# A gated linear recurrence and a low-rank mixer: the first batch's outputs from the diagonal squares, its block totals in place, a bitwise sign, and another order

## The chip, the cores and the metric

The kernel runs on one core of one Trainium2 chip. The metric is device time in microseconds, the median of a few executions; less is better. Engines are named as the profile names them: PE (matmul), PEld (its weight loads), DVE (vector), ACT (scalar), POOL (GpSimd), SP (the queue that issues most DMAs).

## The reference

Two blocks follow each other, all in f32. The first is a complex gated recurrence for 4 batches, 8 heads, 768 steps and 48 channels:

```python
scale = np.minimum(mag, 0.999) / (mag + 1e-06)      # mag = |a_re + i a_im|
a_re_n, a_im_n = (a_re * scale, a_im * scale)
for t in range(S):
    new_re = ar * S_re - ai * S_im                  # ar, ai: a_re_n, a_im_n at t, per channel
    new_im = ar * S_im + ai * S_re
    S_re, S_im = (new_re + outer(k_t, v_t), new_im)
    y[t] = q_t @ S_re
```

Its outputs, heads side by side, are `x` of shape (4, 768, 384) for the second:

```python
h = x.T @ U @ V                                     # per batch, along the sequence; rank 32
u = x + h.T
out = u + np.maximum(u @ w_ch1, 0.0) @ w_ch2        # 384 -> 1536 -> 384
```

## The kernel before

The sequence is cut into chunks of 128 steps, 6 for each batch, 24 in all. Chunks go in groups of two (12 groups); group 0 is worked one chunk at a time. Chunks 0 to 5 are the first batch, groups 0 to 2. From group 3 on (`SPLIT`) sums over time are made from an f32 that is split in two f32r parts.

For each group, `gates` computes the log magnitude (`GL`) and the angle of `a` with ACT's tables and DVE. Part of that is a sign of `a_re` in the tile `n`: for group 0 by DVE as +-0.5, for the others by ACT's Sign. `turns_of` multiplies `n` by arctan minus pi/4 and then scales the product to turns and adds 0.25 (DVE for group 0, ACT for the others). PE sums over time with the triangle `prefix` (`ph`). `within` makes the decay weights inside a chunk (`es`, `ef`). `totals` makes sums of logs over blocks, 32 for each channel (`tot`), which ACT turns into factors. For two heads at once these land in `E`, two heads one under the other, and four DMAs a group place them in `T`, whose rows are the channels once for the cosine half and once for the sine half (rows 0 to 47 and 64 to 111).

For each chunk, `prep` weighs q and k, multiplies them by cosine and sine (`QKC`), transposes them on PE (`tr`), and ACT copies them to `QK`. `chain` computes the chunk's causal weights. `inner` products of q and k in diagonal squares of 32 steps are selected by masks into `DG` (128 x 8 heads x 32). Four DMAs place the squares of `DG` in `AT`, which holds squares of 64. The part of such a square under its diagonal (`corners`) is copied there by ACT, four copies of 32 rows. `dk` is k times v for each half of the chunk; `onward` carries the state from half to half (`GM` for the middle, one buffer; `G` at the end, two). `inside` is then `AT` times v, `before` adds what the state gives, both into two PSUM tiles `y`. Three ACT copies put them into `xo`.

`mixer` takes two chunks at a time, after all six chunks of a batch: `rank`, `mixed`, `uTp`, then `up` and `down` (`few` for the last five mixers, with fewer products). `weights` turns the rows of `w_ch1`, U and V (together) and `w_ch2` from words as loaded into two-part words; each takes two scaling operations (L556), done by DVE for the first four (`EARLY = 4`) and by ACT after that, and three more on DVE.

Nothing is scheduled at run time. Each operation is recorded with its engine, and `ORDER` gives it a place in one sequence, by which all engines' instructions are emitted; each engine works through its own in that order and waits on semaphores. `SPARE` puts matmuls of `ident` with itself (`spare`) ahead of some places: they write a tile that nobody reads.

Of the kernel before, what the change touches and what calls it, by code (L numbers as in the profile page):

```python
# [10 lines left out]
FP = mybir.dt.float32  # L11
# [7 lines left out]
CH = 128  # L19
# [7 lines left out]

ORDER = {
# [9 lines left out]
    ("POOL", "load"): {0: [13], 1.5: [59], 2: [12], 1: [28]},  # L38
    ("DVE", "load"): {1: [40]},
# [6 lines left out]
    ("ACT", "gates"): {0: [0, 7, 6, 11, 16, 21, 23, 36, 53, 43, 44, 45, 55, 58], 1: [14, 8, 22, 29, 30, 37, 46, 54, 48, 49, 52, 57], 2: [127, 104,  # L46
# [10 lines left out]
    ("DVE", "gates"): {0: [10, 9, 17, 25, 27, 63, 24], 1: [15, 26, 33, 35, 38, 64, 41], 2: [117, 144, 151, 186], 4: [261, 313, 314, 352], 6: [427,  # L57
# [10 lines left out]
    ("ACT", "angles"): {0: [78, 87, 92, 93, 100], 1: [84, 101, 107, 111, 110], 2: [197, 202, 220, 236, 232, 238, 239, 246, 248, 249], 4: [363, 376,  # L68
# [5 lines left out]
    ("DVE", "angles"): {0: [81, 82, 90], 1: [85, 88, 103], 2: [201, 231, 245], 4: [375, 395, 419], 6: [563, 567, 571, 592, 599, 600, 636], 8: [672,  # L74
# [5 lines left out]
    ("DVE", "prep"): {0: [91, 102, 112], 1: [116, 124, 138], 2: [240, 254, 257], 3: [241, 275, 306], 4: [402, 407, 425], 5: [424, 432, 464], 6: [608,  # L80
# [159 lines left out]
def kernel(  # L240
# [51 lines left out]
    PAIRED = 5  # L292

    TURN = 0.6
    EARLY, SPREAD = 4, (0,)
    SPLIT = range(3, NG)

    TA, TC, TQ, TK, TF, TH, NTOT = 0, 8, 16, 20, 22, 30, 32
    NP = 128 // R
    PL = H * HC  # L300

    AT_ONCE = (0, 1, 2)
    WP = 768
# [1166 lines left out]
```

## Time and profile before

| | |
|---|---|
| runs | 639.9, 641.53, 642.0 us; median 641.53 |
| profiled execution, span | 641.9 us; no time outside the span is listed for it, and the runs lie around the span |
| busy: PE, PEld, DVE, ACT, POOL | 622.8, 548.0, 509.9, 396.8, 38.7 us |
| mean granted TensorE clock | 0.992 |
| `spare` matmuls | 294 records, 43.9 us busy |
| `AT<-DG`, `T<-E` DMAs | 96 of 32 KB and 48 of 48 KB, median 2.4 and 2.5 us from issue to landing |

A line of a group or of the timeline has the engine, the line of the kernel, the operation, what is written and read, the shapes, and in brackets the idle time of the engine just before and who ended it. An f32 matmul is two records, a transpose or an f32r matmul one. Durations of neighbouring operations of one engine overlap a little, so the time from start to start is shorter than the duration.

### The profile page before, as it was taken

The numbers are of one execution on the slowest core, as the hardware profiler recorded it, in microseconds if no ns is written. First come the engines' busy times: TensorE is split into PE (matmuls) and PEld (weight loads), VectorE is DVE, ScalarE is ACT, GpSimd is POOL, SyncE is SP. The second block draws the span as 40 slices with busy tenths as digits, with TensorE's granted clock in tenths as the row PEclk, the third lists the DMA queues.
The fourth block names the chain that finished last, engine by engine and source line by source line (L and its number), as shares of the span: only waits on it lengthen the run. The fifth ranks groups of instructions, "written<-read, shape, count | busy, mean of one in ns | idle before, by whom it ended". The sixth has DMA issues, their size and how long they took to land.

```text
span 641.9 us, 23713 instructions
## 1 busy us (share of the span) xinstructions
PE 622.8 (97%) x10516; PEld 548.0 (85%) x10516; DVE 509.9 (79%) x923; ACT 396.8 (62%) x765; POOL 38.7 (6%) x79
## 2 busy tenths in 40 slices
PE   8888997999999999999999999999999999999998
PEld 7767776686789988889988989798999998999997
DVE  6998997678999989678877868788999975473743
ACT  7898997788887787876776676687532432102020
POOL 5000000000001010010010100010000000000001
PEclk9999999799999999999999999999999999999999
DMA  7766534745233362333331332611104010000002
GB/s 202 166 148 138 125 70 102 180 119 131 51 66 69 58 126 50 67 69 68 71 77 34 75 74 43 117 37 21 32 20 81 8 42 12 7 1 1 20 1 74
DMA packets 173686, 45.76 MB, mean 71 GB/s; under 512 B 167632, under 2 KB 170384, under 8 KB 173584
## 3 DMA queue, kind: packets, MB, share of 16 engines
q1 hardware_dynamic: 171376, 39.90, 29.4%
q0 software_dynamic: 2208, 4.35, 2.0%
q8 instruction: 82, 1.34, 0.9%
q14 instruction: 20, 0.16, 0.1%
HBM read 33.59 MB, written 4.72 MB: 60 GB/s over the span
## 4 chain that ended last, share of the span: by engine, by line
PE 72%; issue 9%; ACT 7%; DMA 6%; DVE 4%; SPq 3%; POOL 0%; DVEq 0%; ACTq 0%; POOLq 0%
PE down L1284 22%; PE up L1094 11%; PE few L1152 10%; PE y L1012 3%; DMA AT<-DG 3%; PE tr L834 3%; PE dk L973 3%; PE down L1241 3%; ACT gate L374 2%; PE y L1004 2%; PE inner L884 2%; PE inner L881 2%; PE mixed L1066 1%; PE spare L1414 1%; PE tot L718 1%
## 5 line engine op out<-in xcount | busy, mean ns | idle before, releaser
L1094 PE MATMUL up<-uT,w 128*128 128x256 f32 x504 | 116.1, 383 | 0.0
L377 DVE TENSOR_TENSOR QK<-QK,T 112x512 f32<-112x512 f32 (+2 forms) x144 | 101.3, 728 | 7.1 <-PE corners L948 2.6
L1094 PEld LDWEIGHTS up<-uT,w 128*128 128x128 f32 x504 | 93.8, 190 | 12.8
L374 ACT ACTIVATE gate<-gate 128x768 f32<-128x768 f32 (+1 forms) x89 | 70.1, 798 | 8.1 <-DVE GS L768 3.1
L1284 PE MATMUL down<-w,h 128*128 128x192 f32 x396 | 73.5, 331 | 0.0
L845 ACT COPY QK<-tr 112x512 f32<-112x512 f32 x96 | 53.2, 584 | 32.2 <-PE tr L834 31.8
L1284 PEld LDWEIGHTS down<-w,h 128*128 128x128 f32 x396 | 64.1, 190 | 2.7 <-issue 1.5
L1160 ACT COPY h<-few 128x512 f32<-128x512 f32 x30 | 17.3, 586 | 60.9 <-PE few L1152 60.9
L380 DVE TENSOR_TENSOR xo<-down,xo 128x192 f32<-128x192 f32 (+1 forms) x79 | 29.9, 384 | 26.5 <-PE down L1284 26.3
L377 DVE TENSOR_TENSOR QKC<-qk,cs 128x768 f32<-128x768 f32 x48 | 45.4, 952 | 5.2 <-PE tr L834 4.5
L1414 PE MATMUL spare<-ident 128*128 128x128 f32 x294 | 43.9, 295 | 1.4 <-POOL ident masks.py:199 1.4
L1414 PEld LDWEIGHTS spare<-ident 128*128 128x128 f32 x294 | 38.1, 200 | 6.0 <-issue 2.0
L1284 PE MATMUL down<-stage 128*128 128x192 f32 x198 | 37.2, 331 | 0.0
L1152 PE MATMUL few<-gate,w 128*128 128x128 f32 x280 | 35.4, 276 | 0.0
L834 PEld LDWEIGHTS tr<-ident,QKC 64*112 64x112 f32 x768 | 25.9, 130 | 10.7 <-issue 3.3
L834 PE MATMUL tr<-ident,QKC 64*112 64x64 f32 x768 | 33.1, 223 | 1.9 <-ACT QK L845 0.8
L759 POOL DMA_DIRECT2D gate<-F x15 | 11.9, 796 | 379.1 <-DVE F L782 225.3
L1152 PEld LDWEIGHTS few<-gate,w 128*128 128x128 f32 x280 | 33.4, 192 | 0.1
L1284 PEld LDWEIGHTS down<-stage 128*128 128x128 f32 x198 | 32.1, 190 | 1.5 <-DVE stage L1276 0.6
L953 ACT COPY AT<-corners 32x128 f32<-32x128 f32 x96 | 24.2, 255 | 12.1 <-PE corners L948 10.5
L371 ACT ACT_TABLE_LOAD x24 | 30.8, 1283 | 1.1 <-PEq L1454 0.7
L1228 POOL DMA_DIRECT2D out_dram<-xo x32 | 18.5, 606 | 207.2 <-DVE xo L380 119.6
(156 smaller groups left out, 1245.9 us busy)
## 6 DMA issues: line engine op xcount, KB each, us to landing
stage<-in_moe_w_ch_dram SPq DMA_DIRECT2D x12, 768.0 KB, 4.7
gate<-in_a_im_dram SPq DMA_DIRECT2D x24, 192.0 KB, 3.3
gate<-in_a_re_dram SPq DMA_DIRECT2D x24, 192.0 KB, 3.2
VP<-in_v_dram SPq DMA_DIRECT2D x24, 192.0 KB, 3.4
qk<-in_k_dram SPq DMA_DIRECT2D x24, 192.0 KB, 3.3
qk<-in_q_dram SPq DMA_DIRECT2D x24, 192.0 KB, 3.3
AT<-DG SPq DMA_DIRECT2D x96, 32.0 KB, 2.4
T<-E SPq DMA_DIRECT2D x48, 48.0 KB, 2.5
```

Of the source, the lines that this page charges most:

```text
L371: ACT(1.37, rank, lambda: nc.scalar.preload_act_table_set(name), writes=[TABLE])
L374: return nc.scalar.activation(out=o, in_=i, func=f, **kw)
L377: nc.vector.tensor_tensor(out=o, in0=a, in1=b, op=OP.mult)
L380: nc.vector.tensor_tensor(out=o, in0=a, in1=b, op=OP.add)
L834: nc.tensor.transpose(out=get(*ps[r])[0:DQ, h], in_=get(*qkc)[at, h].rearrange("p u d -> p (u d)")[:, 0:DQ], identity=ident[at, at], tile_ ...
L845: nc.scalar.copy(out=to, in_=a)
L953: ACT(0.36, RR, lambda r=r, u=u: nc.scalar.copy(out=get(*ATi).rearrange("p (a u) t -> p a u t", u=2)[r:r + BLK, :, u, BLK:2 * BLK], in_=ge ...
L973: nc.tensor.matmul(out=get(*dk[r])[x:end, h], lhsT=get(*ks)[at, h, x // DP, 0:end - x], rhs=get(*VPi)[at, h], start=True, stop=True, tile_ ...
L1094: nc.tensor.matmul(out=get(*ps)[:, e], lhsT=w1[:, f, (ff + e) * 128:(ff + e + 1) * 128], rhs=get(*uT)[:, f], start=(f == 0), stop=(f == KD ...
L1152: nc.tensor.matmul(out=get(*ps)[:, q], lhsT=w()[:, q * 128:(q + 1) * 128], rhs=v[0](), start=(n == 0 and q == 0), stop=True, skip_group_ch ...
L1284: nc.tensor.matmul(out=get(*to)[:, part], lhsT=x(j), rhs=y[:, j], start=(first and j == 0), stop=(j == KH - 1), skip_group_check=not first)
L1414: nc.tensor.matmul(out=spare[0], lhsT=ident, rhs=ident, start=True, stop=True)
```

## The change

For the chunks of the first batch (`DIRECT` = 6 chunks):

- `y` is computed from `DG` directly: for each head, four matmuls of 32x32 with the diagonal squares and two with the corners, the latter against a copy of v that is shifted by 32 rows and loaded by a DMA of its own into the buffer of `h`; then the state's part, all in one operation (`whole_y`) into one PSUM tile. The four DMAs to `AT` are gone, the corners reach `AT` by one ACT copy, and `xo` is one ACT copy.
- `tot` is computed for every head and both halves of the rows by PE and lands in the layout of `T`; ACT's Exp writes `T`. The DMAs from `E` to `T` are gone.
- A small copy inside `QK` (`back`) is ACT's instead of DVE's, as it was for the later chunks.

For all groups: the sign is one bitwise DVE operation that takes the sign bit of `a_re` and the bits of 1/pi, so that the product is already in turns, and the step that scaled and added 0.25 is gone. The 0.25 comes in with the two `GS` operations (groups from 3 on) or by one more matmul of `prefix` with a constant (groups 0 to 2). `EARLY` is 1 instead of 4. `ORDER` and `SPARE` are new: `SPARE` has 82 matmuls instead of 147. The products with sums of `w_ch2` name all of it as read.

```diff
+INV_PI = 0x3EA2F983
-    EARLY, SPREAD = 4, (0,)
+    EARLY, SPREAD = 1, (0,)
+    DIRECT = NCH
...
+    fourth = column("fourth", 0.25).to_broadcast([128, DM])
...
+        if i < DIRECT:
+            if i == 0:
+                buffer(VS, "h", 1, [128, KF * MC * CH])
+            bi, ci = where(i)
+            SP(c_dma(DM), ("load", (1.45, 2.65)[i] if i < 2 else i + 4.1), lambda: nc.sync.dma_start(
+                out=shifted(i)[BLK:], in_=v[bi, :, ci * CH:(ci + 1) * CH - BLK, :].rearrange("h t d -> t h d")), writes=[VS + (i,)])
...
-            if on_dve:
-                DVE(c_one(W), R1, lambda: nc.vector.tensor_scalar(out=t(n), in0=t(ar), scalar1=0.0, scalar2=0.5, op0=OP.is_ge,
-                                                                  op1=OP.subtract), AR, [N])
-            else:
-                ACT(ca + 0.09, R1, lambda: act(t(n), t(ar), AF.Sign, bias=tiny), AR, [N])
+            DVE(c_one(W), R1, lambda: nc.vector.tensor_scalar(out=t(n).bitcast(U32), in0=t(ar).bitcast(U32), scalar1=0x80000000,
+                                                              scalar2=INV_PI, op0=OP.bitwise_and, op1=OP.bitwise_or), AR, [N])
...
+        def straight(i, R1):
+            ps, tt, at = ("tot", i), ("T", g), (i - first) * DM
+            psum(ps, "T", [128, H, NTOT])
+            def sums():
+                for h in range(H):
+                    for u in range(2):
+                        lo, w = at + h * D, DP if u == 0 else D
+                        parts = [(lo, w)] if u or h < H - 1 else [(lo + D - DP, DP), (lo, D)]
+                        for a, w in parts:
+                            nc.tensor.matmul(out=get(*ps)[u * DP:u * DP + w, h], lhsT=get(*l)[:, a:a + w], rhs=total, start=True, stop=True,
+                                             tile_position=(0, u * DP))
...
+            table(c_act(H * NTOT) - 0.05, R1, lambda: act(get(*tt)[:, i - first].rearrange("p (h b) -> p h b", h=H), get(*ps)[0:DQ],
+                                                          AF.Exp, scale=-1.0), [ps], [tt + (i,)])
...
-            if on_dve:
-                DVE(c_one(W), R2, lambda: nc.vector.tensor_scalar(out=t(z), in0=t(z), scalar1=2.0 / math.pi, scalar2=0.25, op0=OP.mult,
-                                                                  op1=OP.add), [], Z)
-            else:
-                ACT(ca + 0.09, R2, lambda: act(t(z), t(z), AF.Identity, scale=1.0 / math.pi, bias=fourth), [], Z)
...
-                DVE(c_one(DM), R2, lambda: nc.vector.tensor_copy(out=of(a, i), in_=of(z, i)), [zi], [a + (i,)])
+                DVE(c_one(DM), R2, lambda: nc.vector.tensor_scalar(out=of(a, i), in0=of(z, i), scalar1=0.25, scalar2=None, op0=OP.add),
+                    [zi], [a + (i,)])
...
+                PE(0.65, R2, lambda: nc.tensor.matmul(out=get(*ps), lhsT=prefix, rhs=fourth, start=True, stop=False),
+                   [("prefix", 0)], [ps], steps=2)
...
-            nc.scalar.copy(out=o, in_=x) if i >= SPLIT[0] * GC else nc.vector.tensor_copy(out=o, in_=x)
+            nc.scalar.copy(out=o, in_=x)
...
-        for j in range(CH // BLK):
+        direct = i < DIRECT
+        for j in range(0 if direct else CH // BLK):
             js = slice(j * BLK, (j + 1) * BLK)
             to = slice(j % 2 * BLK, j % 2 * BLK + BLK)
             SP(0.2, ("place", i), lambda js=js, to=to: nc.sync.dma_start(out=get(*ATi)[js, :, to], in_=get(*DGi)[js]), [DGi],
...
+        def whole_corners():
+            for h in range(H):
+                for r in (0, HC):
+                    nc.tensor.matmul(out=get(*ps1)[r:r + HC, h], lhsT=q_of(0, (1, HC), at=3 * PL + h * CH + r - BLK),
+                                     rhs=q_of(h, (PL, 2), (1, HB), at=r // 2 + HB), start=True, stop=True, tile_position=(0, r))
...
+        if direct:
+            ACT(0.4, RR, lambda: nc.scalar.copy(out=get(*ATi)[:, :, BLK:2 * BLK], in_=get(*ps1)), [ps1], [ATi])
...
+        def whole_y():
+            for h in range(H):
+                for j in range(CH // BLK):
+                    js = slice(j * BLK, (j + 1) * BLK)
+                    pairs = [(get(*DGi)[js, h], get(*VPi)[js, h]), (get(*ATi)[js, h, BLK:2 * BLK], shifted(i)[js, h])]
+                    for n, (x, v) in enumerate(pairs[:1 + j % 2]):
+                        nc.tensor.matmul(out=get(*y[0])[js, h], lhsT=x, rhs=v, start=(h == 0 and n == 0), stop=(c == 0 and j < 2 and n == j),
+                                         tile_position=(j * BLK, j * BLK), skip_group_check=True)
+            for h in range(H):
+                for r in range(2):
+                    if c or r:
+                        nc.tensor.matmul(out=get(*y[0])[r * HC:(r + 1) * HC, h], lhsT=k_of(h, r * HC, HC),
+                                         rhs=get(*(mid_G if r else ("G", i - 1)))[:, h], start=False, stop=True,
+                                         tile_position=(0, r * HC), skip_group_check=True)
...
+        if direct:
+            PE(1.9, RR, whole_y, [VPi, VSi, ATi, DGi, QK, mid_G] + ([("G", i - 1)] if c else []), y[:1], way=3, takes=[xi], steps=(16 if c else 14) * H)
+            ACT(c_act(DM) - 0.04, RR, lambda: nc.scalar.copy(out=heads(get(*xi)), in_=get(*y[0])), [y[0]], [xi])
+            return
...
-                    PE(0.98, RM, lambda half=half: products(half), reads(half) + [("w2s", 0)],
+                    PE(0.98, RM, lambda half=half: products(half), reads(half) + [("w2s", 0)] + ALL_W2,
```

More of the change, by code (lines that the diff above doesn't have):

```diff
@@ L172 @@
-    ("DVE", "mixing"): {7: [1991, 2012, 2051, 2068, 2070, 1992, 2014, 2086, 2087, 2102, 2103, 2106, 2050]},
-}
-SPARE = {31: 23, 47: 2, 51: 1, 83: 11, 94: 3, 106: 7, 114: 4, 122: 5, 146: 8, 158: 1, 212: 9, 215: 3, 263: 8, 266: 4, 281: 6, 303: 2, 307: 5, 323: 1,
-        349: 2, 371: 7, 383: 1, 388: 1, 420: 6, 426: 4, 435: 1, 460: 3, 463: 1, 467: 1, 476: 6, 484: 2, 506: 1, 507: 1, 532: 1, 573: 1, 575: 2, 577:
-        2, 581: 1}
[9 rows of a table added]
+        ("POOL", "load"): {0: [28], 1: [43], 1.5: [42], 2: [33]},
@@ new lines @@
+        ("DVE", "load"): {1: [71]},
[6 rows of a table added]
+        ("ACT", "gates"): {0: [1, 3, 4, 6, 8, 7, 19, 38, 41, 32, 31, 35, 50, 51], 1: [17, 12, 21, 23, 22, 26, 46, 47, 40, 39, 45, 48], 2: [123, 88,
[9 rows of a table added]
+        ("DVE", "gates"): {0: [5, 9, 10, 13, 20, 66, 16], 1: [18, 25, 29, 24, 27, 69, 57], 2: [100, 136, 154, 192, 164], 4: [242, 266, 288, 300, 299],
[7 rows of a table added]
+        ("ACT", "angles"): {0: [74, 82, 90, 89, 93], 1: [76, 97, 102, 103, 114], 2: [196, 216, 230, 222, 223, 234, 237, 239, 248], 4: [338, 354, 369,
[4 rows of a table added]
+        ("DVE", "angles"): {0: [75, 83], 1: [80, 98], 2: [206, 221, 233], 4: [341, 355, 371], 6: [504, 505, 506, 521, 530, 535, 572], 8: [610, 625,
[5 rows of a table added]
@@ new lines @@
+        ("DVE", "prep"): {0: [63, 94, 105], 1: [112, 119, 126], 2: [170, 240, 254], 3: [199, 257, 272], 4: [313, 370, 382], 5: [361, 388, 412], 6:
[6 rows of a table added]
+        ("ACT", "prep"): {0: [110, 109, 120, 121], 1: [132, 129, 149, 146], 2: [247, 246, 259, 260], 3: [276, 286, 293, 301], 4: [385, 384, 392, 391],
[4 rows of a table added]
+        ("DVE", "rest"): {0: [116, 165, 188, 227, 124, 144, 155], 1: [148, 202, 214, 253, 252, 256, 261, 264], 2: [262, 295, 297, 321, 268, 296, 304,
[8 rows of a table added]
+        ("DVE", "levels"): {0: [122, 133, 147, 134, 143, 163], 1: [150, 160, 184, 166, 171, 201], 2: [267, 280, 290, 275, 285, 316], 3: [314, 339,
[9 rows of a table added]
@@ new lines @@
+        ("ACT", "levels"): {0: [156], 1: [187], 2: [291], 3: [344], 4: [411], 5: [460], 6: [690], 7: [760], 8: [881], 9: [920], 10: [1074], 11:
[8 rows of a table added]
+        ("ACT", "rest"): {0: [219, 243], 1: [238, 263], 2: [329, 353], 3: [378, 398], 4: [458, 478], 5: [483, 497], 6: [728, 753, 736, 735, 787, 785,
[9 rows of a table added]
+        ("ACT", "small"): {0: [499, 515, 555, 548, 542, 568, 533, 596], 1: [660, 709, 726, 767, 721, 689, 777], 2: [895, 1055, 1031, 1053, 960, 995,
[4 rows of a table added]
+        ("DVE", "small"): {0: [511, 516, 513, 665, 674], 1: [615, 663, 616, 747, 770, 773, 799, 834, 840, 867, 912, 888, 856, 907, 890, 908, 889, 926,
[25 rows of a table added]
@@ L684, in within @@
             table(c_act(DM) - 0.05, R1, lambda: act(get(*ef), get(*pf), AF.Exp, scale=-1.0), [pf], [ef])
+        def straight(i, R1):
[9 more added lines that the diff above has]
+                                             tile_position=(0, u * DP))
+            PE(0.9, R1, sums, [l, ("total", 0), ("sums", g)], [ps], way=1, takes=[tt], steps=4 * H + 2)
+            table(c_act(H * NTOT) - 0.05, R1, lambda: act(get(*tt)[:, i - first].rearrange("p (h b) -> p h b", h=H), get(*ps)[0:DQ],
+                                                          AF.Exp, scale=-1.0), [ps], [tt + (i,)])
         def totals():
             e, tt = ("E", g), ("T", g)
-            buffer(e, "E", 1, [128, GC, HH, NTOT])
             ring(tt, "T", TS)
             lo, hi = GROUPS[g]
+            if lo < DIRECT:
+                for part in PARTS[g]:
+                    for i in range(*part):
+                        straight(i, ("gates", part[0]))
+                return
+            buffer(e, "E", 1, [128, GC, HH, NTOT])
             for part in PARTS[g]:
@@ L705, in of_blocks @@
             psum(ps, "T", [128, HH, NTOT])
-            def sums():
-                at = (i - lo) * DM
-                for p in range(HH):
-                    for u in range(2):
-                        h, w = at + (u * HH + p) * D, 64 if u == 0 else D
-                        nc.tensor.matmul(out=get(*ps)[u * 64:u * 64 + w, p], lhsT=get(*l)[:, h:h + w], rhs=total, start=True,
-                                         stop=True, tile_position=(0, u * 64))
             def at_once():
@@ L775, in angles @@
             else:
-                PE(0.65, R2, lambda: nc.tensor.matmul(out=get(*ps), lhsT=prefix, rhs=of(z, i), start=True, stop=not carry),
+                PE(0.65, R2, lambda: nc.tensor.matmul(out=get(*ps), lhsT=prefix, rhs=fourth, start=True, stop=False),
+                   [("prefix", 0)], [ps], steps=2)
+                PE(0.65, R2, lambda: nc.tensor.matmul(out=get(*ps), lhsT=prefix, rhs=of(z, i), start=False, stop=not carry),
                    [zi, ("prefix", 0)], [ps], steps=2)
@@ L803, in gates @@
         return magnitudes, totals, turns, waves
+    VS = ("v shifted", 0)
     def T_of(i, at=0):
@@ L907, in f @@
                 mul(o, x, bass.AP(tensor=tt.tensor, offset=tt.offset, ap=[tt.ap[0], [NTOT, H]] + [list(e) for e in by]))
-            DVE(c_dve(m), rank, f, [("T", group_of(i))], [QK])
+            DVE(c_dve(m), rank, f, [T_at(i)], [QK])
         def scale(rank, of, t, by, m):
@@ L925, in chain @@
         scale(RL, (PL, (HC, H), (8, 8), (1, 8)), TC, ((1, 8), (0, 8)), H * HC)
-        if i >= SPLIT[0] * GC:
-            ACT(c_act(H * HC // 2) - 0.04, RL, back, [], [QK])
-        else:
-            DVE(c_one(H * HC // 2), RL, back, [], [QK])
+        ACT(c_act(H * HC // 2) - 0.04, RL, back, [], [QK])
         yield from inner(1)
         keep(0, near, HB, HB)
-        for j in range(CH // BLK):
+        direct = i < DIRECT
+        for j in range(0 if direct else CH // BLK):
             js = slice(j * BLK, (j + 1) * BLK)
@@ L991, in chain @@
         y, xi = [("y", (i, r)) for r in range(2)], ("xo", i)
-        for r in range(2):
+        VSi = VS + (i,)
+        if direct:
+            y = y[:1] * 2
+            psum(y[0], "Y", [128, H, D], [128, H, DP])
+        for r in () if direct else range(2):
             psum(y[r], "Y", [128, HH, D], [128, HH, CH])
```

61 lines of the change are left out of this document (25 added, 36 removed), and 245 rows, old and new, of the table ORDER.

## The prediction

> **What bounds the kernel now.** I read the busy time by stretches first, cut where the first matmul of the first `up` begins (126.58 us), and the `spare` matmuls alone in the same stretches. The columns are the stretch, its length, busy time and instructions of PE, PEld, DVE, ACT and POOL (in the second fence of PE and PEld), the granted clock, the DMA share and GB/s.
>
> ```profile
> 0.00:126.58 126.58, 111.98 (x2373) 89.53 (x2373) 110.27 (x196) 106.44 (x200) 9.06 (x32) 0.96 0.59 139
> 126.58:641.85 515.27, 510.83 (x8145) 458.46 (x8144) 399.62 (x727) 290.38 (x565) 29.62 (x47) 1.00 0.26 55
> ```
>
> ```profile
> 0.00:126.58 126.58, 43.90 (x294) 38.11 (x294) 0.96 0.59 139
> ```
>
> There are two kernels in one. After 126.58 PE is busy 510.8 of 515.3 us and none of it is filling: that stage is as long as its matmuls. Before it PE does 43.9 us of `spare` work, and the three engines share the stage: DVE is busy 110.3 of 126.6, ACT 106.4. All of the first batch (chunks 0 to 5) lies there. So the end is "when can `up` begin" plus 515 us.
>
> Next, the chain of waits of the first stage (start, us, what): four transfers from `DG` to `AT` stand on it, 16.7 us in all.
>
> ```profile
> 44.33 2.99 DMA AT<-DG
> ...
> 55.70 4.30 DMA AT<-DG
> ...
> 74.45 2.03 DMA AT<-DG
> ...
> 102.77 7.40 DMA AT<-DG
> ```
>
> That is not what they cost, since other engines had work meanwhile. What they cost is idle time of DVE, the fullest engine. In its timeline (start, us, operation, idle time before it and what ended that) four waits follow from them:
>
> ```profile
> 61.95 0.56 DVE L377 TENSOR_TENSOR GM<-G,T 112x384 f32<-112x384 f32 x1 [1.49 <-PE y L1012]
> ...
> 112.72 0.56 DVE L377 TENSOR_TENSOR GM<-G,T 112x384 f32<-112x384 f32 x1 [3.18 <-PE y L1012]
> ...
> 115.88 0.55 DVE L380 TENSOR_TENSOR GM<-GM,dk 112x384 f32<-112x384 f32 x1 [1.73 <-PE dk L973]
> ...
> 122.19 0.36 DVE L767 CAST GS<-gate 128x384 fp32r<-128x384 f32 x1 [1.42 <-ACT gate L374]
> ```
>
> The first two wait for a `y` that waited for `AT`. The third and fourth come behind the second: PE's `dk` ran at half clock, and ACT had stood still 4.1 us for the same `y`. The clock shows in short stretches:
>
> ```profile
> 106.00:108.00 2.00, 1.27 (x67) 0.89 (x66) 1.47 (x4) 1.98 (x5) 0.00 (x0) 1.00 0.89 167
> 108.00:110.00 2.00, 0.32 (x4) 0.22 (x4) 1.54 (x3) 0.58 (x1) 0.00 (x0) 1.00 0.07 24
> 110.00:112.00 2.00, 1.78 (x52) 1.73 (x54) 0.00 (x0) 0.00 (x0) 0.00 (x0) 0.75 0.43 72
> 112.00:116.00 4.00, 4.00 (x83) 3.48 (x84) 1.55 (x3) 2.93 (x9) 0.00 (x0) 0.50 0.30 54
> ```
>
> PE all but stops at 108 for `AT`; from 111.0 to 121.2 the granted clock is 0.5.
>
> **Waits removed.** The first batch has no `AT<-DG` transfer any more (24 fewer) and no `T<-E` (12 fewer; the order also puts two others later); six loads of `v` are added and two loads of `q` come earlier. On SP, where one issue takes about 0.61 us, that is 30 issues fewer before `up`, and what stood behind them moves up. The added loads land in 3.4 us by the row of `VP<-in_v_dram`; five of the six are issued before the second chunk's `y`, the sixth three chunks ahead of its own, so the work of a chunk (over 10 us) hides them; uncovered, one would cost its 3.4. DVE's four waits go: 1.49 + 3.18 + 1.73 + 1.42 = 7.8 us. Bounds: 0 if others take their place; 12.0 if all of DVE's idle time goes (126.6 - 110.3 = 16.3, less 4.3 at the start for the first loads and ACT). I take 7.8.
>
> **DVE work.** Before the first `up`: six copies `QK<-QK` (0.284 us) go to ACT, four conversions of 768 columns (0.55) and two of 384 (0.35) go to ACT by EARLY = 1, two affine steps of `z` (0.356) vanish, three bitwise signs of 768 columns come (0.55, by the integer shift L560 of the same shape). Starts of queued DVE operations are 0.085 us closer than these durations, so the sum is -(1.2 + 2.4 + 0.5) + 1.4 = -2.7 us. The new order puts one `qk` product more (0.87) ahead of `up`: -1.8 us. DVE is 87% full, so I count all of it as path; the bounds are 0 and -2.7. The additions of 0.25 at the `GS` operations keep shape and count: nothing, since L737 does two operations in the 0.95 us in which L380 does one.
>
> **ACT work.** Off: three signs and three affine steps (0.94 each, 5.6), 24 `AT` copies (0.255, 6.1) for six of 256 columns (0.40, 2.4), 18 `xo` copies (0.315, 5.7) for six of 384 columns (0.48, 2.9). On: six `QK<-QK` (2.4), six conversions (4 x 0.91 and, between that and half, 2 x 0.5: 4.6), and 0.13 for each wider Exp into `T` (0.8). Net -4.3 of 106.4 us. It falls by more than DVE, so it does not take over; I count nothing.
>
> **PE work.** The prices, by starts in its timeline:
>
> ```profile
> 73.50 1.30 PE L712 MATMUL tot<-total,GL 128*64 128x32 f32 x32
> 74.73 0.71 PE L1414 MATMUL spare<-ident 128*128 128x128 f32 x4
> ...
> 90.69 0.68 PE L1004 MATMUL y<-VP,AT 64*64 64x48 f32 x32
> 91.31 0.67 PE L1012 MATMUL y<-GM,QK 112*64 112x48 f32 x16
> ...
> 95.36 1.14 PE L973 MATMUL dk<-VP,QKC 64*64 64x48 f32 x64
> 96.44 0.49 PE L1414 MATMUL spare<-ident 128*128 128x128 f32 x2
> ```
>
> One f32 matmul is two records. `tot`: 17 matmuls a chunk for 8, 18 records at (74.73 - 73.50)/32 = 38 ns, +0.7 us. `ph`: one more matmul of 384 columns, +0.7 (81.44 to 82.08 and 83.89 to 84.64 for L776). `y`: 48 matmuls of 32x32 for 16 of 64x64, so 96 records for 32. No row has that shape. The nearest are `inner` (four tiles of 32 columns side by side, 48 moving: 64 records in 0.82 us, 13 ns) and L1004 (four quadrants, 0.62/32 = 19 ns); each pair of odd squares uses one tile twice. I take 14 ns, as its width is that of `inner`: 1.34 us for 0.62, +0.7. Ends: 13 ns if all four overlap, 51 (four times 13) if none do. Together 2.1 us a chunk, 12.7 for six. Against that `spare` falls from 147 matmuls to 82: 130 records at 43.9/294 = 0.149 us, -19.4. PE's total before `up` falls by 6.7 us while the stage shortens by 9.6, so its load stays alike; I count nothing on the path.
>
> Other edits: `DG` is now held until `y` and not until its transfer, with two buffers. The keep of chunk i+2 waits for `y` of chunk i; in the trace `y` of chunk 0 runs at 47.5 and the `inner` of chunk 2 at 61.8, so 14 us cover it. The shifted `v` lives in the buffer of `h`, free again before the mixer starts, which needs all six outputs anyway.
>
> **The second stage.** Its PE work has not one instruction more or less; ACT loses 1.87 us a group, DVE gains 0.55. PE's idle there is 4.4 us. The order is new, the work is not: 515.3, give or take 2.
>
> **Sum.** 126.6 - 7.8 - 1.8 = 117.0; plus 515.3 is 632.3 us of span. The profiled span is 641.9, 0.3 above the median 641.53 of the three runs, which span 639.9 to 642.0. I say 632.0. A measurement of this kernel can tell about 0.3%, 1.9 us, from no change.
>
> **Rivals.** (a) The waits come back under other names. For it: the chain of the stage also holds a 4.10 us load of `gate` at 82.57 and a 6.08 us load of weights at 4.28, and loads queue on SP. Against: those are not followed by DVE waits of that length. Then DVE's own 1.8 us stays and at most two of the 7.8: 638 to 640.
>
> (b) The squares do not overlap; this one ends on the slow side. At 51 ns each a `y` takes 4.9 us for 1.34, +3.6 a chunk, 21 for six. With two thirds of it on the path (each `GM` waits for the `y` before it, the last two lead straight to `up`) the time is 632 + 14 = 646. It decides against the change above 14 + 9600/(6 x 96 x 0.67) = 39 ns a record. For it: four row groups write one bank here. Against: L1004 also writes two row halves into one bank, at 19 ns, and `dk` with a bank for each half is hardly faster, 1.08/64 = 17 ns. The Trainium skill ("TensorEngine Tiling (Array Packing)", Gotcha 1: PSUM Pressure) states that different row tiles cannot access the same PSUM bank simultaneously, which would make this rival the outcome; by L1004 the trace does not bear it out for two row tiles, and no run here shows four.
>
> (c) PE's clock. A spell of 10.2 us at half clock follows the idle at 108, and filling shrinks by 65 matmuls. One spell at full load costs half its length, 5.1; two beyond the forecast give 642, three 647. Against: filling and work together were 106 of 126.6 us by starts and become 98 of 117, the same share, and the only spell follows a wait that is removed. The Trainium skill ("TensorE: Matmul & The Clock Gate", What's actually happening) has the clock fall after an idle window of about 3.4 us; the spell agrees with that, 0.3 us of work in the 2.8 us before 110.2.
>
> **Numbers.** The forecast has a chance of 0.65 (its own range 627 to 637), (a) 0.14, (b) 0.08, (c) 0.10, the rest 0.03 for an order that does nothing. Faster by over 0.3% (under 639.6): the forecast and most of (a), 0.73. Within: 0.09. Slower: 0.18. Low end: 641.9 - 12.0 - 1.8 - 4.4 (PE's idle in the second stage) = 624. High end: 646, which takes in (b) and most of (c).
>
> **What would show it.** Right: first `up` near 117 us; no DVE wait over 1.5 us on `y`; the `y` squares at 12 to 20 ns a record; clock 1.00 from 100 to 122; 515 us after `up`. Wrong: `up` at 123 or later with new long waits (a), squares near 50 ns (b), stretches at clock 0.5 (c), or a second stage over 518.

## The result: slower by 2.7%

The changed kernel takes 657.96 us (median of four runs, 655.14 to 658.47), the kernel before 640.71 us (four runs beside them). The ratio is 1.027, with a 95% interval of 1.024 to 1.030. The forecast was 632.0 us with a range of 624 to 646, so its sign was wrong. Ratios below are to executions of the kernel before that were made beside those of each experiment, 80 in all; 0.01 is 6.4 us. Some executions fall into a slower state with a lower clock, and the ratios leave those out.

### The profile page after: what moved, and what is told of

It is laid out like the page before. It is cut to its first block, busy times and chain, and to the rows that moved or that the text cites. A ratio compares the mean times of both kernels' runs of the same rounds, so it can differ in the third digit from the quotient of the medians.

```text
span 656.7 us, 24382 instructions
## 1 busy us (share of the span) xinstructions
PE 632.0 (96%) x10890; PEld 551.2 (84%) x10890; DVE 511.8 (78%) x919; ACT 379.8 (58%) x725; POOL 37.1 (6%) x79
## 3 DMA queue, kind: packets, MB, share of 16 engines
q1 hardware_dynamic: 168208, 39.40, 29.4%
q8 instruction: 85, 1.39, 0.9%
## 4 chain that ended last, share of the span: by engine, by line
PE 83%; issue 7%; DVE 5%; ACT 3%; DMA 1%; POOL 0%; SPq 0%; DVEq 0%; POOLq 0%; ACTq 0%
PE down L1331 22%; PE up L1141 16%; PE few L1199 10%; PE tr L849 4%; PE dk L997 3%; PE inner L899 3%; PE down L1288 2%; PE y L1055 2%; PE inner L896 2%; PE y L1042 2%; PE tot L733 2%; PE mixed L1113 2%; PE y L1032 1%; PE uTp L1126 1%; PE rank L1094 1%
## 5 line engine op out<-in xcount | busy, mean ns | idle before, releaser
L374 DVE TENSOR_TENSOR QK<-QK,T 112x512 f32<-112x512 f32 (+2 forms) x144 | 102.8, 729 | 9.9 <-PE inner L899 3.5
L849 PEld LDWEIGHTS tr<-ident,QKC 64*112 64x112 f32 x768 | 26.6, 132 | 11.3 <-issue 5.6
L371 ACT ACTIVATE h<-up 128x512 f32<-128x512 f32 x42 | 24.9, 596 | 15.8 <-PE up L1141 15.7
L911 DVE COPY_PREDICATED DG<-mask,inner 128x128 f32<-128x128 int32 (+1 forms) x72 | 24.2, 341 | 11.2 <-PE inner L896 8.8
L997 PEld LDWEIGHTS dk<-VP,QKC 64*48 64x48 f32 (+1 forms) x1408 | 25.4, 127 | 8.9 <-issue 4.9
L997 PE MATMUL dk<-VP,QKC 64*48 64x48 f32 (+1 forms) x1408 | 29.0, 217 | 3.3 <-issue 3.2
L1130 ACT COPY uT<-uTp 128x384 f32<-128x384 f32 x12 | 5.7, 478 | 45.0 <-PE uTp L1126 45.0
```

Of the source, the lines that this page charges most:

```text
L371: return nc.scalar.activation(out=o, in_=i, func=f, **kw)
L374: nc.vector.tensor_tensor(out=o, in0=a, in1=b, op=OP.mult)
L849: nc.tensor.transpose(out=get(*ps[r])[0:DQ, h], in_=get(*qkc)[at, h].rearrange("p u d -> p (u d)")[:, 0:DQ], identity=ident[at, at], tile_ ...
L911: nc.vector.copy_predicated(out=to, mask=part(mask[:, n], "p").unsqueeze(1).to_broadcast(list(to.shape)), data=a if t == BLK else a.rearra ...
L997: nc.tensor.matmul(out=get(*dk[r])[x:end, h], lhsT=get(*ks)[at, h, x // DP, 0:end - x], rhs=get(*VPi)[at, h], start=True, stop=True, tile_ ...
```

## The profile after

First the busy time by stretches, cut at the first `up` (135.75 us; 126.58 before), and the `spare` matmuls alone (columns as in the prediction's fences).

```profile
0.00:135.75 135.75, 118.21 (x2746) 92.18 (x2746) 108.66 (x185) 101.14 (x176) 7.30 (x32) 0.91 0.60 133
135.75:656.70 520.95, 513.76 (x8145) 459.07 (x8144) 403.14 (x735) 278.64 (x549) 29.81 (x47) 1.00 0.25 52
```

```profile
0.00:135.75 135.75, 27.37 (x164) 23.94 (x164) 0.91 0.60 133
```

The first stage is 9.2 us longer and the second 5.7. DVE and ACT are less busy than before (108.7 and 101.1 for 110.3 and 106.4), as forecast. PE's `spare` work has fallen by 16.5 us, and yet PE is busy 6.2 us more: everything else it does has grown from 68.1 to 90.8 us. The granted clock of the stage is 0.91 for 0.96.

Next, what DVE waits for in the first stage (total, times, longest), the four largest:

```profile
DVE xo L377 <- PE mixed L1113: 4.7, 1, 4.7
DVE QKC L374 <- PE dk L997: 4.7, 2, 3.4
DVE gate L633 <- ACT gate L371: 2.8, 1, 2.8
DVE QK L374 <- PE inner L899: 2.7, 3, 1.5
...
DVE GM L374 <- PE y L1047: 1.3, 2, 0.8
```

The long waits of `GM` on `y` are gone, as forecast; 1.3 us is left. In their place DVE waits for PE elsewhere: for `dk`, `inner` and `mixed`.

In the chain of waits of the first stage a piece called "issue" has grown, from 5.8% before to 11.3%:

```profile
34.24 1.00 issue
...
58.06 1.04 issue
...
66.29 2.87 issue
...
100.61 1.45 issue
...
117.95 1.62 issue
```

The profile shows nothing that PE waits for there. Below, a "stop without a wait" is a standstill of PE of 0.3 us or more that its timeline puts down to "issue": 8.9 us in seven stops here, 2.9 in four before. Of those shown, the third stop is inside one `dk`, after 9 of its 64 records. Behind the last of these lies the longest stretch at half clock (0.50 in the column after POOL):

```profile
121.70:135.40 13.70, 13.53 (x171) 9.19 (x167) 8.21 (x14) 4.66 (x8) 0.00 (x0) 0.50 0.72 167
```

With the spells at 9.1 (6.8 us) and 70.5 (3.4) it makes 23.9 us at half clock; before it was 10.2.

## The experiments

My first theory, A, was that PE's instructions are the limit: the stops of the kind "issue" all fall at the same instruction of every 256, and PE has about 750 instructions more ahead of `up`. The rivals: B, the new order is bad; C, PE's clock falls because there are fewer fillers; D, PE's real work lies on the path, which my prediction had counted at nothing.

### The new order, fillers, squares, and more records before

All four kernels are one edit each. `e1` takes `ORDER` and `SPARE` from the kernel before. The others:

```diff
e2 -SPARE = {30: 15, 36: 2, ...
   +SPARE = {30: 23, 36: 2, ...
e3  def whole_y():
   -    for h in range(H):
   +    for h in range(3 if c else H):
e4  (kernel before, inside(), chunks 0 to 5)
   +    for x in range(0, D, 16):
   +        to = slice(x, x + 16)
   -    nc.tensor.matmul(out=get(*y[u])[side(r, u), p], ... rhs=get(*VPi)[at, h], start=(p == 0), ...
   +        nc.tensor.matmul(out=get(*y[u])[side(r, u), p, to], ... rhs=get(*VPi)[at, h, to], start=(p == 0 and x == 0), ...
```

> All operations of the changed kernel, emitted in the order of the kernel before: an operation that both have keeps its old place, a new one takes the place of what it replaces (the whole y that of the last y, the one corner copy that of the last of four, the Exp into T that of the Exp into E, the shifted v right behind v), and the spare matmuls are the old 147. Theory A (PE's instructions arrive in blocks of 256, and the change puts three blocks more ahead of the first up; the stalls and the half-clock spells behind them are the loss): PE has 2877 matmul records ahead of up for 2746 in the changed kernel, a block more, so up comes no earlier than about 131 us and the total is 645 to 658. Theory B (the new order is what is bad): up at 117 to 122, total 632 to 638. Both: the second stage, whose order is then the old one, takes 515 to 516 us again for 521, if its loss is one of order.

Measured: 661.77 us, ratio 1.032 (1.027 to 1.038), `up` at 139.4. That spoke for A, but stops without a wait were 2.5 us for 8.9, with a block of instructions more. And the run was spoilt by something that no theory had: first `dk` at 37.4 us for 28.0, behind a 4.8 us wait of PE. It is run again below (`e1b`).

> The changed kernel with 23 spare matmuls at the start for 15, as before. Theory C (PE's clock: fewer fillers let it fall): the idle time of 2.7 us at 7.1 us and the half-clock spell from 9.1 to 15.9 are gone, the first dk comes 1.5 to 3 us earlier, and up with it, total 654 to 656.5. Theory A: the start gets faster, but what follows it goes by instruction blocks and is as slow as it was; up within 1 us of 135.7, total 657 to 658.5.

Measured: 655.45 us, ratio 1.023 (1.018 to 1.028), `up` at 130.7, first `dk` 1.9 us earlier, no half clock before 69 us. The total is C's; `up` came 5.1 us earlier, more than C's 1.5 to 3, as the later spells are shorter too (13.7 us at half clock in all). The interval touches that of the changed kernel (1.024 to 1.030), so the 2.5 us are likely and not sure.

> The changed kernel with 18 of the 48 square matmuls of each y in chunks 1 to 5 (heads 0 to 2 only; the outputs of the other heads lack their part inside the chunk). That is 300 matmul records, 600 instructions, 2.3 blocks less, and at 15.8 ns a record 0.95 us less of PE time in each of five chunks, 4.7 in all. Theory A: up comes earlier by more than the PE time, 6 to 10 us (126 to 130), stalls without a wait fall from 8.9 us to under 5, total 648 to 652. If only PE's time counts: up at 131 to 133, total 653 to 655. If neither (order, clock): 656 to 658.

Measured: 648.65 us, ratio 1.011 (1.007 to 1.016), `up` at 123.65: 12.1 us earlier for 4.7 us of matmuls. Stops without a wait are 5.2 us, not under 5: A's total, but hardly by A's way. What is gone beside the matmuls is half clock, 23.9 us down to 3.4.

> The kernel before with the 16 square matmuls of y cut in three pieces of 16 columns each for chunks 0 to 5: same products, 96 records for 32 as in the changed kernel, 384 records or 768 instructions (3 blocks) more ahead of up, nothing else changed. At 11 to 19 ns a record it is 0.4 to 1.2 us of PE time a chunk. Theory A: new stalls without a wait at every 256th instruction, up later by 5 to 10 us (131 to 137), total 646 to 651. If only PE's time counts: two thirds of it on the path, 2 to 5 us, total 642.5 to 645.5. If PE has room: 640 to 642.

Measured: 656.96 us, ratio 1.024 (1.020 to 1.029), `up` at 140.1. The total is above all three ranges, and the stops without a wait are only 2.0 us. The timeline shows why: the narrow pieces cost as much as the wide ones.

```profile
47.11 2.78 PE L1006 MATMUL y<-VP,AT 64*64 64x16 f32 x96 [0.33 <-DMA AT<-DG]
```

2.78 us for 96 records of 16 columns is 29 ns each, where 32 of 48 columns took 0.67 us, 21 ns. So `e4` added 2.1 us of PE time a chunk (12.6 in all) and not 0.4 to 1.2, and moved `up` by 13.5. The stage has 27.3 us at half clock for 10.2, which can be up to 8.5 of the 13.5; whether the longer matmuls brought these spells on is not shown. With three blocks more and fewer stops, A was in trouble.

### Part by part, in the old order

The kernel before, its order and spares, with one part of the change's diff each; new operations stand where those they replace stood.

> The kernel before, its order and its 147 spare matmuls, with one part of the change: y from the diagonal squares (the squares, the corners and xo in their new form, the shifted load of v, no transfers from DG to AT). In the run of all new operations in the old order the y and the corners cost PE 4.8 and 4.1 us more at full clock than before. Theory D (PE's real work before up lies on the path nearly whole, since the spare matmuls run whether there is time or not, and the waits it replaces were only partly on it): up at 130 to 135 us, total 645 to 650. Theory of the prediction (the four waits go, PE's work is hidden): up near 119, total 633 to 636. Theory A (instruction blocks): 256 more records, two blocks, up later with new stalls without a wait of 3 us or more in all.

Measured: 648.13 us, ratio 1.007 (1.004 to 1.011), `up` at 129.4; stops without a wait 4.7 us (2.9 before). The total is in the range of theory D, and `up` a little ahead of it. The clock is no rival here: the two executions with a mean clock of 1.00 take 647.17 and 647.8 us, the five of the kernel before with 1.00 beside them 639.85 to 642.41. So it costs about 6 us at full clock, two thirds of the 9.2 us by which PE's `y` and corners grew (16.17 and 7.09 us, for 11.36 and 2.75 in `q4` below).

> The kernel before, its order and spares, with one part of the change: the block totals of the first three groups made by PE in their final layout, Exp into T, no transfers from E to T. PE has 108 records and about 3.2 us more. Theory D: up later by 2 to 4 us, total 642.5 to 645. Theory of the prediction: no more than 0.5 us either way, 640 to 642.

Measured: 643.16 us, ratio 1.000 (0.997 to 1.003), `up` at 122.6 with the clock at 1.00 throughout. In the total the prediction's step holds for this part: 3.3 us of PE work came and 12 transfers went, and the time is the same. That the one pays for the other is my reading.

> The kernel before, its order and spares, with the rest of the change: the bitwise sign on DVE, no affine step, the 0.25 by one more matmul of prefix for chunks 0 to 5 and in the GS operations after that, EARLY = 1, the small copy in QK by ACT. PE has 12 records and about 5 us more before up; ACT is 6.6 us less busy, DVE 2.7. Theory D: up later by 3 to 6 us. Theory of the prediction: up earlier by 1 to 3 us. The second stage went from 515.3 to 519.2 us with all new operations in the old order; if the sign and the 0.25 do that, it is 518 to 520 here and 515 to 516 in the other two parts. Totals: 645 to 650 by D, 639 to 643 by the prediction's.

Measured: 657.15 us, ratio 1.022 (1.017 to 1.026), above both. As in `e1`, PE stands still early:

```profile
19.17 0.81 PE L769 MATMUL ph<-fourth,prefix 128*128 128x384 f32 x2
24.67 1.52 PE L771 MATMUL ph<-gate,prefix 128*128 128x384 f32 x2 [4.68 <-DVE gate L734]
```

`EARLY = 1` puts conversions of weights on ACT at places where DVE had done them, ahead of ACT's part of the first angles. So this run does not price the sign; `q4` and `q5` do.

> The changed kernel with 23 spare matmuls at the start and none after that, for 82 in all; no work is left out. Theory D with fillers that stand only where PE would wait: up within 3 us of the 130.7 of the run with 23 at the start, if the clock holds. If fillers too lie on the path: up earlier by up to 15 us, total 640 to 650. If the clock falls for want of them: half-clock spells of more than 25 us and up at 138 or later, total 660 or more.

Measured: 666.47 us, ratio 1.036 (1.032 to 1.041), `up` at 141.0, 58 us at half clock.

```profile
0.00:140.96 140.96, 113.43 (x2628) 88.33 (x2629) 109.01 (x185) 101.24 (x176) 7.30 (x32) 0.79 0.57 126
```

PE is busy 113.4 us against 114.5 in `e2`, although 19 us of spares are gone: what they took, real work at a clock of 0.79 takes in their place. In this kernel the fillers pay for themselves.

### PE's work and the late groups

`q4` does the bitwise sign and the moved 0.25 only `if g in SPLIT`. `q5` adds one matmul:

```diff
+                PE(0.65, R2, lambda: nc.tensor.matmul(out=get(*ps), lhsT=prefix, rhs=one, start=True, stop=False),
+                   [("prefix", 0)], [ps], steps=2)
```

`m1` drops that matmul from the changed kernel, adds 0.25 to `z` on DVE in groups 0 to 2, and computes corners for `[r + BLK:r + HC]` only. `yt` is the y part and the totals together in the old order, with those corners.

> The kernel before, its order and spares, with the bitwise sign on DVE, no affine step by ACT and the 0.25 in the GS operations for groups 3 to 11 only; chunks 0 to 5 are as before. PE has no instruction more or less anywhere. ACT has 1.87 us less a group, DVE 0.55 more, nine groups. If the sign part is what made the second stage longer (521.6 us in the run of that part alone, 515.3 before): first up within 1 us of 126.6, second stage 518 to 522, total 644 to 648. If not (the prediction's step): 515 to 517 and a total of 640 to 642.5.

Measured: 645.0 us, ratio 1.003 (1.000 to 1.006), second stage 518.3 us. The surprise is the first stage, whose work is that of before: `up` at 121.5, 5.1 us earlier.

```profile
0.00:121.52 121.52, 107.64 (x2373) 86.67 (x2373) 110.68 (x197) 104.72 (x198) 9.67 (x32) 1.00 0.62 143
```

The clock is 1.00. So the profile of before, on which the prediction rests, was of an execution with a half-clock spell, and the 5.1 us are half of the spell's 10.2. The second stage is what the text expected if the sign makes it longer (518 to 522). Of DVE's four waits (7.8 us) these are left here:

```profile
DVE GM L377 <- PE y L1018: 1.8, 2, 1.1
...
DVE GM L380 <- PE dk L979: 0.9, 1, 0.9
```

> The kernel before, its order and spares, with one more matmul of prefix for chunks 0 to 5, with a constant 1 (whole turns, which change no phase). 12 records, 5.0 us of PE by the runs above (0.42 each), nothing else. Theory D (PE's work before up is on the path): up later by 3 to 5 us, second stage unchanged, total 643 to 647 by the profile. The prediction's step (hidden behind the other engines, spares take the slack): up within 1 us of 126.6, total 640 to 643. Instruction blocks cannot do it: 24 instructions are a tenth of one.

Measured: 645.18 us, ratio 1.003 (1.001 to 1.005), clock 1.00, `up` at 123.4, 1.9 us behind `q4`. PE's `ph` costs 4.2 us more (13.14 for 8.97), and 0.3% is 1.9 us: just under half of it is in the time. The interval allows from 0.3 to 3.4 us.

> The changed kernel in its own order with less PE work before up, computing the same: 0.25 added by one DVE operation on z in groups 0 to 2 for the six matmuls of prefix with a constant (PE 5 us less, DVE 1.8 more); the corners computed for the 32 rows of each half that are used, for 64 (33 ns a record now; 13 ns was the price of before's, side by side in four columns; with two I estimate 17 to 25, 1.5 to 3 us less); 23 spares at the start. Theory D: up 5 to 8 us before the 130.7 us of the run with 23 spares, 123 to 126, total 646 to 650, since the second stage keeps its 521 to 524. If PE's work is not on the path: 130 to 132, total 653 to 656.

Measured: 660.53 us, ratio 1.027 (1.024 to 1.031), `up` at 134.2. D failed here: less PE work, and no gain. A look at where the matmul stood settles part of it. The first two lines are of the changed kernel, the third is of `m1`:

```profile
48.42 0.91 PE L784 MATMUL ph<-fourth,prefix 128*128 128x384 f32 x2
50.45 0.91 PE L786 MATMUL ph<-gate,prefix 128*128 128x384 f32 x2 [0.22 <-DVE gate L749]
...
50.55 0.88 PE L788 MATMUL ph<-gate,prefix 128*128 128x384 f32 x2 [2.03 <-DVE gate L754]
```

In the changed kernel the matmul with the constant, and fillers behind it, ran while PE would have waited for `gate`; L754 is the addition on DVE that replaces it. In groups 0 and 1 PE waits 4.5 us ahead of these `ph` in `m1` (1.60, 0.83 and 2.03) for 0.7 in the changed kernel, so most of the 5 us of PE work came back as waiting. The corners did get cheaper (0.70 us for 32 records, 1.12 in the changed kernel), but PE's stops without a wait are 9.9 us, the most of all runs, DVE has four operations more and ACT six. What eats the rest is open.

> A version meant to be better than both: before's order, spares and sign, with y from the diagonal squares, the totals in place, and the corners computed for the 32 used rows only. By the parts run alone: totals -4.0 us, y +2.9, corners -1.5 to -3: up at 122 to 124, second stage 517, total 639 to 641 by the profile, 0 to 3 us under before. If the parts do not add (with all three parts in the old order up was at 139.4, 6 later than their sum): 645 or more.

Measured: 655.23 us, ratio 1.019 (1.015 to 1.023), `up` at 136.1 with 10.2 us at half clock. The parts do not add: 0.7% and 0.0% alone, 1.9% together, even with narrower corners.

### Instructions or time

`spare` matmuls of four times the columns, a quarter as many (`s1`, `s3`, `s4`), or of half the columns, twice as many (`s2`):

```diff
-        nc.tensor.matmul(out=spare[0], lhsT=ident, rhs=ident, start=True, stop=True)
+        nc.tensor.matmul(out=spare[0][:, 0:w], lhsT=ident, rhs=ident[:, 0:1].to_broadcast([128, w]), start=True, stop=True)
s2
+        for x in (0, 64):
+            nc.tensor.matmul(out=spare[0][:, x:x + 64], lhsT=ident, rhs=ident[:, x:x + 64], start=True, stop=True)
```

> The kernel before with every four spare matmuls of 128 columns as one of 512 (a constant column, broadcast; nobody reads the result): 147 become 51, 384 PE instructions or 1.5 blocks fewer ahead of up, about the same PE time. Theory A (instruction blocks): fewer stalls at block ends, 0 to 3 us faster, total 638 to 642 where before has 641 to 643. Theory D (PE's time): within 1 us of before.

> The changed kernel with 23 spares at the start (655.45 us so far, ratio 1.023), and every four spares of 128 columns as one of 512: 90 become 36, 216 instructions or 0.85 of a block fewer. Theory A: faster by 2 to 6 us, ratio 1.013 to 1.020. Theory D: the same, ratio 1.021 to 1.025.

Measured: `s1` 640.88 us, ratio 1.000 (0.996 to 1.003); `s3` 658.72 us, ratio 1.026 (1.022 to 1.031), `up` at 130.2 for 130.7. The saving was smaller than the texts say: four at a time, the 147 spares become 78 and the 90 become 42 (138 and 96 matmul records fewer in the traces), so 1.1 and 0.75 blocks less. Nothing moved, and for `s3` theory A had asked for 2 to 6 us. A falls as the main cause; a part of it is not excluded.

> The kernel before with every spare matmul of 128 columns as two of 64: 588 PE instructions, 2.3 blocks, more ahead of up, nearly the same PE time. Theory A: first up later by 4 to 12 us, with stalls at block ends and half-clock spells behind them, total 646 to 656. Theory D: within 2 us of before, 640 to 644.

Measured: 667.57 us, ratio 1.033 (1.028 to 1.039). The ratio goes by two executions, of 661.41 and 663.77 us; the profiled one took 672.07. The two halves cost twice the whole, so this is a test of D and not of A:

```profile
0.00:153.22 153.22, 85.45 (x588) 81.70 (x588) 0.95 0.52 120
```

85.5 us of `spare` for 43.9, and no stop without a wait at all. In the profiled execution 41.5 us more of PE time made the kernel 31 us longer. (In the first 26 us 98 of these records follow each other at 213 ns, about twice the usual distance.) The other two are 21 us longer, and their PE time is not on record; at 112 ns, the distance at full clock, 294 records more are 33 us. By this estimate about two thirds is in the time.

> The kernel before with the block totals in place (ratio 1.000 alone) and the 147 spares as 51, 1.5 blocks fewer: the version that could beat both. Theory A: ratio 0.994 to 0.998. Theory D: 0.999 to 1.002.

Measured: 639.76 us, ratio 0.999 (0.996 to 1.002), `up` at 120.5, the earliest of all (here too the spares became 78, not 51). No version is shown to beat the kernel before; this one is level with it.

### Order or operations, and copies in place of transfers

> All operations of the changed kernel in the order and with the 147 spares of the kernel before, but EARLY = 4 as before, so that the conversions stay with DVE. No wait of 4.8 us at 19.5 us any more, first dk near 29 us. Theory D (new PE work, 16 us at full clock, six to seven tenths of it in the time, less the transfers' waits): up at 129 to 135, total 648 to 654, ratio 1.010 to 1.020; the new order then accounts for the rest, 4 to 10 us. If the order is what is bad: ratio under 1.005. If it has no part: 1.025 or more.

Measured: 653.02 us, ratio 1.019 (1.015 to 1.022), first `dk` at 29.4. So the operations alone, at their old places, cost 11.9 us. The new order with its fewer spares and EARLY = 1 accounts for the other 5.3, by difference. The clock does not make the 11.9: the execution with the highest mean clock, 0.999, takes 651.49 us, and the eleven of the kernel before with 1.00 beside it take 638.25 to 641.5. Below, busy times of the stage here, and then what DVE waits for:

```profile
0.00:135.84 135.84, 127.37 (x2876) 105.60 (x2877) 110.46 (x190) 96.93 (x170) 8.71 (x32) 0.96 0.55 127
```

```profile
DVE F L792 <- ACT F L371: 4.1, 3, 2.4
DVE QK L374 <- PE inner L899: 3.0, 3, 2.4
...
DVE gate L749 <- ACT gate L371: 2.2, 2, 1.6
DVE DG L911 <- PE inner L899: 1.8, 1, 1.8
DVE QKC L374 <- PE dk L997: 1.6, 1, 1.6
```

DVE is as busy as in `q4` (110.5 and 110.7 us), and the stage is 14.3 us longer (a spell of 10.2 us at half clock is in it). It waits for `ph` (by way of ACT's `F`), `inner` and `dk`: for PE, which runs its new work between them.

> The kernel before with the block totals in place, the 147 spares as 51 (both as in the run with ratio 0.9987), and the diagonal squares put into AT by four GpSimd copies of 32 x 256 a chunk for chunks 0 to 5, in place of the four DMAs; y stays at 16 square matmuls. GpSimd is busy 9 of 126 us there. PE's work stays. If the transfers' waits (7.8 us of DVE's idle time in the profile of before) were worth what the prediction said: up 3 to 7 us earlier than 120.5, ratio 0.990 to 0.995. If a copy takes over a microsecond or DVE slows beside it: 0.998 or more.

Measured: 643.28 us, ratio 1.005 (1.003 to 1.007), `up` at 124.4. A copy takes 1.36 us:

```profile
L949 POOL COPY AT<-DG 32x256 f32<-32x256 f32 x24 | 32.7, 1364 | 69.4 <-DVE DG L909 68.4
```

Four of them in a row take 5.5 us, longer than three of the four transfers that the prediction showed.

## Why the prediction was wrong, point by point

**PE's work "I count nothing on the path".** This is the step that failed. It set fillers off against work: 12.7 us more work, 19.4 us fewer fillers, load alike. What the runs showed: with every filler in place and DVE as busy as before, the new operations make the kernel 11.9 us longer (`e1b`), and DVE's waits are then for PE's `ph`, `inner` and `dk`. Where PE's time alone changes, about half to two thirds of it is in the total (`q5`, `s2`), and about as much for the `y` part at full clock (`p1`); in `e3` and `e4` spells at half clock go and come with it. Taking fillers away gained nothing (`f1`). My reading is that a filler stands where PE would wait anyway, and a `tot`, a corner or a square stands between two operations of DVE. `m1` shows the limit of that: the constant's matmul stood in a wait too, and its removal brought little. `p2` has its PE work for nothing.

**The sizes.** Between `q4` and `e1b`, by busy time of each tile up to `up`, in the same order and with the same fillers:

| | before's form | new form | predicted | measured |
|---|---|---|---|---|
| `y` | 11.36 | 16.18 | +4.2 | +4.8 |
| `tot` | 5.09 | 8.40 | +4.2 | +3.3 |
| `ph` | 8.97 | 12.59 | +4.2 | +3.6 |
| corners | 2.75 | 7.40 | 0 | +4.7 |

The squares were right: in the changed kernel 95 records in 1.52 us, 16 ns, so rival (b) falls, though four row groups write one bank. The corners I missed. Their instructions are as many as before, but 64 rows wide in two places where they were 32 rows wide in four, and a record costs 33 ns for 12 from start to start:

```profile
L954 PE MATMUL corners<-QK 112*32 112x32 f32 x192 | 2.7, 199 | 0.0
```

```profile
L962 PE MATMUL corners<-QK 112*64 112x32 f32 x192 | 7.4, 224 | 1.4 <-issue 0.6 <-ACT gate L371 0.5 <-DVE DG L911 0.2
```

(The first line is of `q4`, the second of `e1b`: busy us, then mean ns of one; the matmuls overlap, so the busy time tells, not the mean.) Half of those rows are not read by anyone. Together +16.4 us for 12.7. These sums are not made by the 10.2 us at half clock of `e1b`: in `p1` (3.4 us) `y` and corners take 16.17 and 7.09.

**DVE's four waits, 7.8 us.** The mechanism was right, they are gone. The size was not: it was read from one execution. In `q4`, with the same first stage at full clock, 2.7 us of them are left to win. The other 5 hang on one late transfer and the spell behind it. In the profiled execution of before (first line) PE stops inside a `y` for squares that reach `AT` late, by the transfer of 7.40 us, and then runs at half clock; in `q4` (second line) the same `y` runs in one piece:

```profile
110.22 0.67 PE L1004 MATMUL y<-VP,AT 64*64 64x48 f32 x28 [1.40 <-DMA AT<-DG]
...
108.50 0.79 PE L1010 MATMUL y<-VP,AT 64*64 64x48 f32 x32 [0.95 <-DMA gate<-in_a_re_dram]
```

Of the 80 executions of the kernel before beside these runs, 32 have a mean clock of 1.00 and span 636.3 to 640.5 us, 16 have 0.992 (that of the profile) or less and span 641.1 to 645.7, and 32 lie between. So a spell as long as the profile's is the rarer case, and what it goes with is no wait that the transfers make each time.

**Span and time.** The forecast took the span for the time. In these 80 executions the time is 1.7 to 3.3 us longer than the span (median 1.9). So the profiled execution took about 644 us, some 2 us above the median that the prediction put it beside.

**The second stage, "515.3, give or take 2".** It became 520.95. Ten profiles with the old sign have 515.3 to 519.3 us, four with the new sign in the old order 518.3 to 521.7 (`q4`, `e1b`, `e1`, `p3`), six with the new order too 520.9 to 525.0. So some 2 us go with the sign and 2 to 3 with the order; these are single executions. For the sign, `q4` is 0.3% longer in total with this change alone. The prediction had ACT's loss and DVE's gain there at nothing.

**Rivals.** (a) came true in a form I had not priced: waits came back, for PE's new work and not for transfers. (c) came true in part: three stretches at half clock where I had one, at most 7 us more by these two profiles. The clock of 100 to 122 us that I asked for was 0.5 from 121.7 on.

**The sum that holds:** 11.9 us for the operations and 5.3 for the order, of which the start with 15 spares for 23 is perhaps half (`e2`). How the 11.9 come out of 16.4 us of PE work, the transfers' waits and the work off DVE and ACT was not measured term by term. Open are why y and totals together cost more than apart, and what eats the rest of the gain in `m1`.

## What to carry to other kernels

Filler work and real work of an engine cannot be set off against each other: price an added operation by whether another engine's next step waits behind it, even where the engine does much filling. Before pricing a wait, look whether the execution shown has a spell of low clock or a transfer slower than its fellows, and compare with one that has none. A change of an instruction's shape is a change of its price, even where the count stays: check each touched operation's form in the built kernel against its row.

## What the runs showed of the hardware

- Below some size, fewer columns did not make an f32 matmul cheaper. With 128x128 weights, records of `spare` start 112 ns apart at full clock whether they have 128 columns (kernel before, first line) or 64 (`s2`, second line); with 512 columns it is 433 ns (`s1`). (The rows shown hold slower records too.) Pieces of 16 columns at 29 ns a record for 48 at 21 (`e4`) say the same for 64x64 weights.

```profile
14.98 2.72 PE L1414 MATMUL spare<-ident 128*128 128x128 f32 x22
...
28.73 5.12 PE L1415 MATMUL spare<-ident 128*128 128x64 f32 x44
```

- Instructions arrive by a DMA queue of their own, in blocks of 16 KB (changed kernel):

```profile
q8 instruction: 85, 1.39, 0.9%
```

85 packets are 1.39 MB. The seven stops without a wait of the changed kernel lie at the same place in every 256 of PE's instructions and last up to 2.87 us, with a block landing 1.2 to 1.6 us before PE goes on. The Trainium skill ("Runtime: NRT & Kernel Launch", Instruction fetch mechanics) has blocks of 16 KiB, which agrees, and calls the cost of crossing one "mostly hidden"; here the crossings hold PE for 8.9 us of the first stage after the change, though fewer instructions (`s1`, `s3`) did not make the kernel faster.
